# RMS norm with its sums on every partition, the norm of the next chunk begun at tile 2, and three id lists in place of one

## The chip, the cores and the metric

One Trainium2 chip, one core of it. The metric is the device time of one execution in microseconds (us), lower is better.

TensorE does the matmuls; VectorE, ScalarE and GpSimd (POOL in the profile) the elementwise work; SyncE (SP) issues most of the DMAs, POOL the indirect ones. Each of them works through its own instructions in order.

## What is computed

The input x has 8 batches of 3072 tokens with 256 features. Three blocks follow one another; cut to what matters:

```python
X = np.fft.rfft(x, axis=1)                       # Fourier block, per batch
Yr = Xr @ w_r - Xi @ w_i + b_r
Yi = Xr @ w_i + Xi @ w_r + b_i
Y = soft_threshold(Yr, 0.01) + 1j * soft_threshold(Yi, 0.01)
x = np.fft.irfft(Y, n=3072, axis=1)              # now 24576 tokens x 256

rms = np.sqrt(np.mean(x * x, axis=-1, keepdims=True) + 1e-06)
xn = x / rms * rms_g                             # RMS norm
x = (silu(xn @ w_gate) * (xn @ w_val)) @ w_out   # gated MLP, 1536 wide

expert_idx = np.argmax(normalize(x) @ normalize(expert_emb).T / tau, axis=1)
out[mask_e] = gate_w * (np.maximum(x[mask_e] @ w1[e], 0.0) @ w2[e])   # 8 experts, 1024 wide
```

## The kernel before, in words

Products are made in float16 with a high and a low part of each operand, so most products are three matmuls (high times high, high times low, low times high).

**Startup** prepares constants and weights and the Fourier block of batch 0. The last DMA of the Fourier block (`gen_A`) writes its result to G in memory.

**Chunk stage.** There are 64 chunks of 384 tokens (CT), 8 to a batch, c = 0 to 7. For each chunk, `load_gt` loads a piece of G, a chunk ahead. `norm_steps` makes from it, with 24 small matmuls (L819), the activations v (features on partitions, tokens along the row), squares them into q on ScalarE, adds the two halves on POOL and splits the sum into bfloat16 parts (two halves of q, and ql). The sums over features come from nine matmuls with a column of ones at L843, in `ms`; they stand with tokens on partitions. From them VectorE computes the reciprocal root on 128x3 values (m, mri, mry, mrt), two DMAs through memory (rd, then R) bring it as one row to all 128 partitions, VectorE multiplies v by R, ScalarE writes xnh and POOL xnl, the two halves of the normalized activations. v, q, R, xnh and xnl have one buffer each.

A chunk then has 12 tiles (`gv`, L887): 12 matmuls of 128x384 with xnh and xnl into two of the four PSUM banks of this kind, a SiLU on ScalarE (th), the product hf on VectorE (L154), hh on ScalarE and hl on VectorE. Three output tiles follow (`out_tile`, L921), 108 matmuls of 128x264. `route_steps` is the router of the chunk before: positions of each token among its expert's, then three indirect DMAs from POOL (L992) that scatter the 384 token ids into the list idl in memory; posi holds the places, rowi (L967) the ids. The rows themselves go to x2d.

What sets the order: `norm_steps` and `route_steps` are generators. `tick` advances both, twice in a gv tile and at each step of an output tile; `pump` advances `gen_A` of the next batch, which runs beside the chunks c = 0 to 4 of a batch (chunks with FFT work; 5 to 7 are plain). The norm of the next chunk is begun at tile f = 6:

```python
if more and f == 6:
    self.ns = self.norm_steps(*chunks[i + 1])
```

The scheduler then puts each engine's instructions in a fixed order.

**Expert stage** (`phase_C`). Twelve jobs, eight experts and four floating ones that take what is over, 52 units of work. The token ids of a unit come from idl (loads idx0, idx1, idx and fidx), an indirect DMA from POOL gathers the rows, and a transposing DMA on SP brings them into xt. The weights of a job come as w1f and w2f on SP; `gen_expert` takes their maxima on VectorE (rm, L1075 and L1078), scales and splits them. In each unit ScalarE makes eh and VectorE el from the first product; the second product is at L1164. `prep` runs beside the units: it loads job j once `self.done >= j - 3`, then makes the weights of job j - 1.

`prefill` writes a number past the last token into all of idl, early in startup (six DMAs, pfill).

## Time and profile before

| | before |
|---|---|
| runs | 4216.44, 4218.2, 4221.3 us; median 4218.2 |
| the profiled execution | 4221.03 us, its span 4219.1 us |
| granted TensorE clock, mean | 0.982 |
| startup / chunk stage / expert stage | 158.6 / 2971.8 / 1088.7 us |
| busy: TensorE | 3997.2 us (95%) |
| busy: VectorE, ScalarE, POOL | 2516.2 us (60%), 1929.2 us (46%), 1211.0 us (29%) |

The profile is of one execution. Busy time is the time in which an engine executes something; waiting instructions are not in it. A clock of 1 is the full 2.4 GHz. In the rows, L843 is line 843 of the kernel before, `out<-in` names the tiles written and read, x is a count, and a bracket behind a row holds the idle time before it and what ended it.

### The profile page before, as it was taken

To read this page: it belongs to the slowest core of one execution; us is meant where nothing else is said; L and a number is where in the kernel's file an instruction comes from. 1 tells how busy PE (TensorE), PEld (TensorE's weight loads), DVE (VectorE), ACT (ScalarE), POOL (GpSimd) and SP (SyncE) were. 2 spreads that over 40 slices of the span, in tenths; PEclk is the share of its full clock that TensorE was granted. 3 is DMA by queue.
4 is the path that set the end of the run, shared out by engine and by line. 5 is a ranking of instruction groups with operands and counts; after the bars stand their busy time and mean duration, and the time that the engine had idled before them with its cause. 6 is when DMAs were issued, how large, how long until landed. Compare 5 with 4: busy or idle time off the path is not lost.

```text
span 4219.1 us, 82489 instructions
## 1 busy us (share of the span) xinstructions
PE 3997.2 (95%) x31534; PEld 2835.7 (67%) x31534; DVE 2516.2 (60%) x7667; ACT 1929.2 (46%) x4326; POOL 1211.0 (29%) x1451
## 2 busy tenths in 40 slices
PE   8889999998999999999999999999999999999998
PEld 6566666766766676677667667666666666666666
DVE  7566577667756766676676576666663343333432
ACT  5544454455446444544544454444442333333332
POOL 3123113321322232132123213222233333333332
PEclk9899999999999999999999999999999999999999
DMA  7221122112212221321132123211124343333431
GB/s 239 61 55 45 31 52 56 44 35 56 55 33 50 60 48 30 62 50 38 41 59 52 29 43 56 77 27 29 22 58 116 91 112 95 94 91 91 95 76 46
DMA packets 337697, 263.42 MB, mean 62 GB/s; under 512 B 232789, under 2 KB 304259, under 8 KB 337298
## 3 DMA queue, kind: packets, MB, share of 16 engines
q1 hardware_dynamic: 311954, 206.39, 21.6%
q0 software_dynamic: 25344, 51.73, 4.7%
q8 instruction: 248, 4.06, 0.5%
q14 instruction: 151, 1.24, 0.1%
HBM read 133.02 MB, written 77.79 MB: 50 GB/s over the span
## 4 chain that ended last, share of the span: by engine, by line
PE 57%; DMA 16%; DVE 15%; issue 4%; ACT 4%; POOL 3%; SPq 1%; DVEq 0%; POOLq 0%; ACTq 0%
PE gv L887 21%; PE gv L1148 11%; PE ms L1164 6%; PE out L1164 6%; DMA R<-rd 5%; PE out L921 4%; DMA rd<-mry 3%; DMA idl<-rowi,posi 3%; PE ms L540 3%; DVE hf L154 3%; DVE hl L150 2%; PE gv L921 2%; ACT hh L158 1%; DMA at<-A 1%; POOL xnl L150 1%
## 5 line engine op out<-in xcount | busy, mean ns | idle before, releaser
L887 PE MATMUL gv<-xnh,wgvh 128*128 128x384 f16 x3072 | 1007.5, 328 | 52.0 <-DVE hf L154 30.3
L887 PE MATMUL gv<-xnl,wgvh 128*128 128x384 f16 x3072 | 1007.7, 328 | 22.4 <-POOL xnl L150 22.4
L887 PE MATMUL gv<-xnh,wgvl 128*128 128x384 f16 x3072 | 1007.6, 328 | 0.0
L887 PEld LDWEIGHTS <-wgvh 128*128 128x128 f16 x6144 | 586.3, 98 | 431.3 <-issue 79.5
L158 ACT ACTIVATE hh<-hf 128x384 f16<-128x384 f32 x768 | 400.6, 522 | 629.3 <-DVE hf L154 628.1
L150 DVE TENSOR_TENSOR hl<-hf,hh 128x384 f16<-128x384 f32 x768 | 461.3, 601 | 282.3 <-ACT hh L158 279.6
L921 PEld LDWEIGHTS <-hh 128*128 128x128 f16 x4608 | 455.0, 99 | 74.1 <-issue 0.5
L154 DVE SCALAR_TENSOR_TENSOR hf<-gv,kh,th 128x384 f32<-128x384 f32 x768 | 469.7, 612 | 35.0 <-PE gv L887 22.4
L1148 PE MATMUL gv<-xt,w1h 128*128 128x512 f16 (+1 forms) x1664 | 484.2, 375 | 0.8 <-ACT w1h L158 0.8
L992 POOL DMA_INDIRECT idl<-rowi,posi x192 | 204.4, 1064 | 970.4 <-DMA idl<-rowi,posi 398.8
L158 ACT ACTIVATE th<-gv,kg 128x384 f32<-128x384 f32 x768 | 435.3, 568 | 59.1 <-PE gv L887 58.6
L887 PEld LDWEIGHTS <-wgvl 128*128 128x128 f16 x3072 | 301.0, 98 | 235.3 <-issue 41.2
L154 DVE SCALAR_TENSOR_TENSOR el<-gv,eh 128x512 f16<-128x512 f32 (+1 forms) x416 | 276.5, 669 | 282.9 <-ACT eh L158 282.9
L921 PE MATMUL out<-woh,hl 128*128 128x264 f16 x1536 | 428.8, 279 | 0.4 <-DVE hl L150 0.4
L921 PE MATMUL out<-woh,hh 128*128 128x264 f16 x1536 | 429.1, 279 | 0.0
L921 PE MATMUL out<-wol,hh 128*128 128x264 f16 x1536 | 428.9, 279 | 0.0
L158 ACT ACTIVATE eh<-gv 128x512 f16<-128x512 f32 (+1 forms) x416 | 240.8, 580 | 284.9 <-PE gv L1148 284.2
L1164 PEld LDWEIGHTS <-eh 128*128 128x128 f16 x3200 | 313.4, 98 | 56.7 <-issue 0.6
L1170 POOL DMA_INDIRECT out<-o,xg x200 | 202.1, 1010 | 487.1 <-ACT o L158 239.5
L1148 PE MATMUL gv<-xt,w1l 128*128 128x512 f16 (+1 forms) x832 | 311.0, 374 | 0.0
L150 POOL TENSOR_TENSOR xnl<-v,xnh 128x384 f16<-128x384 f32 x128 | 116.2, 928 | 662.3 <-ACT xnh L158 637.6
L1148 PEld LDWEIGHTS <-w1h 128*128 128x128 f16 x1664 | 163.8, 99 | 147.2 <-issue 5.4
(339 smaller groups left out, 7462.4 us busy)
## 6 DMA issues: line engine op xcount, KB each, us to landing
x2d<-row SPq DMA_DIRECT2D x64, 387.0 KB, 5.8
G<-go SPq DMA_DIRECT2D x192, 128.0 KB, 1.8
gt<-G SPq DMA_DIRECT2D x64, 384.0 KB, 4.5
xc<-in_x SPq DMA_DIRECT2D x60, 384.0 KB, 6.0
R<-rd SPq DMA_DIRECT2D x64, 192.0 KB, 4.2
w1f<-in_moe_w SPq DMA_DIRECT2D x12, 1024.0 KB, 9.5
w2f<-in_moe_w SPq DMA_DIRECT2D x12, 1024.0 KB, 6.5
xt<-xg SPq DMA_TRANSPOSE x200, 3.2
```

The costliest lines, as they stand in the source:

```text
L150: (eng or self.nc.vector).tensor_tensor(out=out, in0=a, in1=b, op=op)
L154: self.nc.vector.scalar_tensor_tensor(out=out, in0=a, scalar=s, in1=b, op0=op0, op1=op1)
L158: self.nc.scalar.activation(out=out, in_=a, func=func, **kw)
L540: nc.tensor.matmul(ps, lhsT=x[u][z][:, dc], rhs=W[w][:, dc, z * D:z * D + D], start=(k == 0), stop=(k == 11))
L887: nc.tensor.matmul(p_, lhsT=self.wgv[q][u][:, dc, f * P:(f + 1) * P], rhs=xn[w][:, dc], start=(k == 0), stop=(k == 5))
L921: nc.tensor.matmul(ps, lhsT=a[:, k * P:(k + 1) * P], rhs=w[:, f], start=(n == 0), stop=(n == 3 * NF - 1))
L992: nc.gpsimd.indirect_dma_start(out=self.idl, out_offset=bass.IndirectOffsetOnAxis(ap=pi[:, k:k + 1], axis=0), in_=ri[:, k:k + 1], in_offse ...
L1148: nc.tensor.matmul(ps, lhsT=w1[1 + a][:, dc, f * P:(f + 1) * P], rhs=xt[:, 2 * z + dc, 0:n], start=(k == 0), stop=(k == 5))
L1164: nc.tensor.matmul(ps, lhsT=a[:, f, k * P:(k + 1) * P], rhs=w2[1 + z][:, f], start=(j == 0), stop=(j == 3 * NFE - 1))
L1170: nc.gpsimd.indirect_dma_start(out=self.out, out_offset=bass.IndirectOffsetOnAxis(ap=xg[:, k, 257:258], axis=0), in_=o, in_offset=None, bo ...
```

## The change

Four parts. The sums over features come from three matmuls of a 128x128 matrix of ones with the 128x384 squares, so that each partition holds the sum of every token; the reciprocal root is then computed on 128x384 values, and the two DMAs through memory fall away. The norm of the next chunk begins at tile 2, in the last chunk of a batch still at tile 6. The id list becomes three, one for each of the scatters; whoever reads ids loads from all three and takes the least. Prefill is moved to the end of startup, and `prep` loads the weights of a job without waiting for `done`, and waits with the making of job j - 1 until `done >= j - 4`.

```diff
@@ -822,58 +822,50 @@
             yield 1
             yield 1
         self.tt(q[:, 0], q[:, 0], q[:, 1], ALU.add, nc.gpsimd)
-        for _ in range(5):
-            yield 1
-        ps = self.ps("ms")
-
-        def by_k(a):
-            return a.rearrange("p (n k) -> p n k", k=3)
-
-        qh = [q[:, i].bitcast(BF16).rearrange("p (n k t) -> p n k t", k=3, t=2)[:, :, :, 1] for i in range(2)]
-        ql = pb.tile([P, CT], BF16, tag="ql", name="ql", bufs=1)
-        self.tt(by_k(q[:, 1]), by_k(q[:, 0]), qh[0], ALU.subtract, nc.gpsimd)
-        yield 1
-        yield 1
-        self.tt(by_k(ql), by_k(q[:, 1]), qh[1], ALU.subtract, nc.gpsimd)
         for _ in range(3):
             yield 1
-        parts = qh + [by_k(ql)]
-        for k in range(3):
-            for i, z in enumerate(parts):
-                nc.tensor.matmul(ps[:, k:k + 1], lhsT=z[:, :, k], rhs=self.onesb[:, 0:1], start=(i == 0), stop=(i == 2))
+
+        qh = [q[:, i].bitcast(BF16).rearrange("p (n t) -> p n t", t=2)[:, :, 1] for i in range(2)]
+        ql = pb.tile([P, CT], BF16, tag="ql", name="ql", bufs=1)
+        self.tt(q[:, 1], q[:, 0], qh[0], ALU.subtract, nc.gpsimd)
+        for _ in range(2):
+            yield 1
+        self.tt(ql, q[:, 1], qh[1], ALU.subtract, nc.gpsimd)
+        for _ in range(6):
+            yield 1
+
+        ps = self.ps("ms")[:, 0:CT]
+        for i, z in enumerate(qh + [ql]):
+            nc.tensor.matmul(ps, lhsT=self.onesb, rhs=z, start=(i == 0), stop=(i == 2))
         yield 1
-        m = self.sm(pb, "m", 3)
-        self.ts(m, ps[:, 0:3], self.eb[b], 1e-30, ALU.add, ALU.max)
+        m, t = q[:, 0], q[:, 1]
+        self.ts(m, ps, self.eb[b], 1e-30, ALU.add, ALU.max)
         yield 1
-        y = yield from self.one(self.rsqrt_steps(pb, m, 3, "mr"))
-        self.ts(y, y, 32768.0)
+
+        y = pb.tile([P, CT], F32, tag="R", name="R", bufs=1)
+        nc.vector.tensor_scalar(out=t.bitcast(I32), in0=m.bitcast(I32), scalar1=1, scalar2=None, op0=ALU.logical_shift_right)
         yield 1
-
-        rd = self.rd[(b * NCH + c) % 2]
-        nc.sync.dma_start(out=rd.rearrange("(p k) -> p k", k=3), in_=y)
-        R = pb.tile([P, CT], F32, tag="R", name="R", bufs=1)
-        nc.sync.dma_start(out=R, in_=rd.unsqueeze(0).broadcast_to([P, CT]))
-        for _ in range(4):
+        nc.vector.tensor_scalar(out=y.bitcast(I32), in0=t.bitcast(I32), scalar1=-1.0, scalar2=1597463007.0, op0=ALU.mult, op1=ALU.add)
+        yield 1
+        for _ in range(3):
+            self.tt(t, y, y)
+            yield 1
+            self.stt(t, t, -0.5, m, ALU.mult, ALU.mult)
+            yield 1
+            self.stt(y, t, 1.5, y, ALU.add, ALU.mult)
             yield 1
         xh = pb.tile([P, 2, CT], F16, tag="xnh", name="xnh", bufs=1)
         xl = pb.tile([P, 2, CT], F16, tag="xnl", name="xnl", bufs=1)
         for dc in range(2):
-            self.tt(v[:, dc], v[:, dc], R)
+            self.stt(v[:, dc], v[:, dc], 32768.0, y, ALU.mult, ALU.mult)
             yield 1
         for dc in range(2):
             self.act(xh[:, dc], v[:, dc])
+            yield 1
+        for dc in range(2):
             self.tt(xl[:, dc], v[:, dc], xh[:, dc], ALU.subtract, nc.gpsimd)
-            yield 1
         self.xn[b, c] = (xh, xl)
-
-    def one(self, g):
-
-        while True:
-            try:
-                next(g)
-            except StopIteration as e:
-                return e.value
-            yield 1
+        yield 1
 
     def gv(self, b, c, f):
         nc, pb = self.nc, self.pb
@@ -990,7 +982,7 @@
         nc.vector.tensor_copy(pi, ps_)
         for k in range(3):
             nc.gpsimd.indirect_dma_start(
-                out=self.idl, out_offset=bass.IndirectOffsetOnAxis(ap=pi[:, k:k + 1], axis=0),
+                out=self.idl[k], out_offset=bass.IndirectOffsetOnAxis(ap=pi[:, k:k + 1], axis=0),
                 in_=ri[:, k:k + 1], in_offset=None)
         yield
         y = yield from self.rsqrt_steps(pb, ssx, 3, "rx")
@@ -1043,17 +1035,28 @@
 
         nc = self.nc
         n = -(-(NE * self.CAP + FUNIT) // (6 * P)) * 6 * P
-        self.idl = self.dram.tile([n, 1], I32, name="idl")
+
+        self.idl = [self.dram.tile([n, 1], I32, name=f"idl{k}") for k in range(3)]
         self.x2d = self.dram.tile([self.NT + 1, ROW], I32, name="x2d")
         w = n // P
         t = pf.tile([P, 512], F32, tag="dq", name="pfill", bufs=2)[:, 0:w // 6].bitcast(I32)
         nc.gpsimd.memset(t, self.NT)
-        for j in range(6):
-            nc.sync.dma_start(out=self.idl.rearrange("(j p w) o -> j p (w o)", p=P, j=6)[j], in_=t)
+        for l in self.idl:
+            for j in range(6):
+                nc.sync.dma_start(out=l.rearrange("(j p w) o -> j p (w o)", p=P, j=6)[j], in_=t)
         z = pf.tile([1, ROW], I32, name="zrow")
         nc.gpsimd.memset(z, 0)
         nc.gpsimd.memset(z[:, ROW - 1:ROW], BIGID)
         nc.sync.dma_start(out=self.x2d[self.NT:self.NT + 1], in_=z)
+
+    def load_ids(self, pool, name, shape, src, bufs=1):
+
+        t = [pool.tile([P] + shape, I32, tag=f"{name}{k}", name=f"{name}{k}", bufs=bufs) for k in range(3)]
+        for o, l in zip(t, self.idl):
+            self.nc.sync.dma_start(out=o, in_=src(l))
+        for k in (1, 2):
+            self.tt(t[0], t[0], t[k], ALU.min)
+        return t[0]
 
     def expert(self, pw, w1src, w2src):
 
@@ -1114,8 +1117,7 @@
 
         n = EARLY * UNIT
         self.ts(self.cntb[:, 0:1], self.cntb[:, 0:1], float(n), op0=ALU.max)
-        idx = self.pw.tile([P, n // P], I32, name="idx0")
-        self.nc.sync.dma_start(out=idx, in_=self.idl[0:n].rearrange("(p k) o -> p (k o)", p=P))
+        idx = self.load_ids(self.pw, "idx0", [n // P], lambda l: l[0:n].rearrange("(p k) o -> p (k o)", p=P))
         n4 = UNIT // P
         self.early = [self.unit_load(self.pw, idx[:, n4 * k:n4 * k + n4], n4) for k in range(EARLY)]
 
@@ -1236,21 +1238,20 @@
 
         nc = self.nc
         p0 = nc.sync.value_load(self.tb[0:1, col], min_val=0, max_val=NE * self.CAP)
-        idx = pc.tile([P, FUNIT // P], I32, tag="fidx", name="fidx", bufs=bufs)
-        nc.sync.dma_start(out=idx, in_=self.idl[bass.ds(p0, FUNIT)].rearrange("(p k) o -> p (k o)", p=P))
-        return idx
+        return self.load_ids(pc, "fidx", [FUNIT // P], lambda l: l[bass.ds(p0, FUNIT)].rearrange("(p k) o -> p (k o)", p=P), bufs=bufs)
 
     def phase_C(self, pc, pw, w0, w1):
         nc = self.nc
         spp = self.SLOT // P
         per = self.SLOT // UNIT
         n4 = UNIT // P
-        idl = self.idl[0:NE * self.CAP].rearrange("(e r) o -> e (r o)", e=NE)
         lo = EARLY * UNIT
-        idx0 = pc.tile([P, spp - lo // P], I32, name="idx1")
-        nc.sync.dma_start(out=idx0, in_=idl[0, lo:self.SLOT].rearrange("(p k) -> p k", p=P))
-        idx = pc.tile([P, NE - 1, spp], I32, name="idx")
-        nc.sync.dma_start(out=idx, in_=idl[1:NE, 0:self.SLOT].rearrange("e (p k) -> p e k", p=P))
+
+        def by_expert(l):
+            return l[0:NE * self.CAP].rearrange("(e r) o -> e (r o)", e=NE)
+
+        idx0 = self.load_ids(pc, "idx1", [spp - lo // P], lambda l: by_expert(l)[0, lo:self.SLOT].rearrange("(p k) -> p k", p=P))
+        idx = self.load_ids(pc, "idx", [NE - 1, spp], lambda l: by_expert(l)[1:NE, 0:self.SLOT].rearrange("e (p k) -> p e k", p=P))
 
         jobs = []
         for e in range(NE):
@@ -1289,11 +1290,11 @@
             yield
             for j in range(2, len(jobs) + 1):
                 if j < len(jobs):
-                    while self.done < j - 3:
-                        yield
                     load_w(j)
                     yield
                 if j > 2:
+                    while self.done < j - 4:
+                        yield
                     yield from self.gen_expert(pw, ws[j - 1])
                     self.ready = j - 1
 
@@ -1363,13 +1364,13 @@
         self.ns = sa
         for _ in range(3):
             next(ga)
-        self.prefill(wp)
         for _ in ga:
             pass
         for _ in self.rs:
             pass
         for _ in self.load_c(False):
             pass
+        self.prefill(wp)
         self.rate = None
 
     def main(self):
@@ -1378,7 +1379,6 @@
         self.hpend = None
         self.ns = self.rs = self.xs = iter(())
         self.rcred, self.rate = 0.0, None
-        self.rd = [self.dram.tile([CT], F32, name=f"rd{i}") for i in range(2)]
         self.G = [self.dram.tile([96, T2, 512], F16, name=f"G{b}") for b in range(2)]
         es = ExitStack()
         self.pa = es.enter_context(tc.tile_pool(name="pa", bufs=1, side="right"))
@@ -1446,7 +1446,7 @@
                 if more and edge and f == 3:
                     drain(ga)
                     self.load_gt(*chunks[i + 1])
-                if more and f == 6:
+                if more and f == (6 if edge else 2):
                     self.ns = self.norm_steps(*chunks[i + 1])
                 self.gv(b, c, f)
                 pump(1.95 * rg)
```

On POOL, the router's scatters of a plain chunk of the first batch and the norm that shares the chunk with them (row writes the token number, rowi the ids, q and ql the squares, xnl the low half of the activations). Before:

```order
L1018 TENSOR_SCALAR row<-kr 128x3
L992 DMA idl<-rowi,posi 211200x1 x3
L967 TENSOR_SCALAR rowi<-kr 128x3
L150 TENSOR_TENSOR q<-q 128x384 x2
L150 TENSOR_TENSOR ql<-q 128x384
L150 TENSOR_TENSOR xnl<-v,xnh 128x384 x2
```

and now:

```order
L1010 TENSOR_SCALAR row<-kr 128x3
L150 TENSOR_TENSOR q<-q 128x384
L984 DMA idl_1245<-rowi,posi 211200x1
L150 TENSOR_TENSOR q<-q 128x384
L984 DMA idl_1246<-rowi,posi 211200x1
L984 DMA idl_1247<-rowi,posi 211200x1
L150 TENSOR_TENSOR ql<-q 128x384
L959 TENSOR_SCALAR rowi<-kr 128x3
L150 TENSOR_TENSOR xnl<-v,xnh 128x384 x2
```

The first q stands ahead of the scatters, the second among them, and ql ahead of rowi.

On VectorE, gv tiles 7 to 9 of the fourth chunk of the second batch (c and at, yv and yw belong to the FFT of the batch after). Before:

```order
L154 SCALAR_TENSOR_TENSOR hf<-gv,kh,th 128x384
L154 SCALAR_TENSOR_TENSOR c_81<-ms,c_81 128x4x128
L150 TENSOR_TENSOR hl<-hf,hh 128x384
L144 TENSOR_SCALAR c_81<-c_81 128x8x64
L154 SCALAR_TENSOR_TENSOR hf<-gv,kh,th 128x384
L144 TENSOR_SCALAR at<-at,eq 128x1024
L150 TENSOR_TENSOR hl<-hf,hh 128x384
L154 SCALAR_TENSOR_TENSOR yv<-ms,k_8555,bsc_8551 128x256
L146 TENSOR_SCALAR yw<-yv,lam,nlam 128x256
L154 SCALAR_TENSOR_TENSOR hf<-gv,kh,th 128x384
```

and now, from the second of these hf to the third:

```order
L154 SCALAR_TENSOR_TENSOR hf<-gv,kh,th 128x384
L154 SCALAR_TENSOR_TENSOR q<-q 128x384
L144 TENSOR_SCALAR at<-at,eq 128x1024
L154 SCALAR_TENSOR_TENSOR yv<-ms,k_8424,bsc_8420 128x256
L154 SCALAR_TENSOR_TENSOR R<-q,R 128x384
L146 TENSOR_SCALAR yw<-yv,lam,nlam 128x256
L150 TENSOR_TENSOR q<-R 128x384
L150 TENSOR_TENSOR hl<-hf,hh 128x384
L154 SCALAR_TENSOR_TENSOR hf<-gv,kh,th 128x384
```

Three wide operations of the reciprocal root (q, R, q) stand between two hf that had none of them between.

On SP, the beginning of the expert stage, weight loads against the transposes of the units (xt; ISA rows are bookkeeping). Before:

```order
L1132 DMA_TRANSPOSE xt<-xg 128x4x128 x20
L1064 DMA w1f<-in_moe_w 128x2x1024
L1064 DMA w2f<-in_moe_w 128x8x256
L1132 DMA_TRANSPOSE xt<-xg 128x4x128 x18
L1064 ISA
L1064 DMA w1f<-in_moe_w 128x2x1024
L1132 DMA_TRANSPOSE xt<-xg 128x4x128 x4
L1064 ISA
L1064 DMA w2f<-in_moe_w 128x8x256
```

and now:

```order
L1067 DMA w1f<-in_moe_w 128x2x1024
L1067 DMA w2f<-in_moe_w 128x8x256
L1134 DMA_TRANSPOSE xt<-xg 128x4x128 x20
L1067 ISA
L1067 DMA w1f<-in_moe_w 128x2x1024
L1067 ISA
L1067 DMA w2f<-in_moe_w 128x8x256
L1134 DMA_TRANSPOSE xt<-xg 128x4x128 x26
```

The loads of the same job stand twenty transposes earlier, and the pair that was split by four transposes stands together.

## Rows read from the trace of the kernel before

**Rows 1.** Busy by stretch: length, busy us PE, PEld, DVE, ACT, POOL; clock, DMA share, GB/s.

```profile
158.61:3130.45 2971.84, 2815.45 (x23652) 2027.84 (x23652) 1976.19 (x6394) 1460.47 (x3449) 776.71 (x977) 0.98 0.21 45
3130.45:4219.10 1088.65, 1055.10 (x7321) 716.09 (x7318) 429.47 (x959) 383.77 (x703) 388.37 (x394) 0.99 0.37 91
635.50:697.60 62.10, 57.15 (x508) 41.92 (x506) 41.36 (x128) 25.32 (x62) 18.58 (x24) 0.95 0.27 57
```

**Rows 2.** What TensorE waits for: total us, times, longest us.

```profile
PE gv L887 <- DVE hf L154: 30.3, 35, 2.8
PE ms L843 <- POOL q L150: 26.0, 22, 5.2
PE gv L887 <- POOL xnl L150: 22.4, 60, 0.7
PE out L1164 <- DVE el L154: 20.9, 7, 7.1
PE ms L843 <- POOL ql L150: 17.2, 26, 0.9
PE gv L887 <- ACT xnh L158: 12.9, 5, 8.6
PE ms L540 <- DVE go L154: 12.4, 6, 2.3
PE ms L511 <- DVE go L154: 12.2, 10, 4.2
...
PE ms L511 <- DVE at L144: 7.8, 2, 7.5
```

**Rows 3.** Timeline of POOL in a plain chunk: start us, duration, instruction, [idle before, releaser].

```profile
2718.82 0.96 POOL L992 DMA_INDIRECT idl<-rowi,posi  x1 [6.19 <-DMA idl<-rowi,posi]
2723.43 0.22 POOL L967 TENSOR_SCALAR rowi<-kr 128x3 int32<-128x3 int32 x1 [3.65 <-DMA idl<-rowi,posi]
2723.63 1.88 POOL L150 TENSOR_TENSOR q<-q 128x384 f32<-128x384 f32 x2
```

**Rows 4.** Timeline of TensorE in the same stretch.

```profile
2724.66 0.21 PE L843 MATMUL ms<-onesb,q 128*128 128x1 bf16 x1 [5.21 <-POOL q L150]
```

**Rows 5.** Timeline of VectorE in the output stage of a chunk with FFT work.

```profile
792.92 1.03 DVE L150 TENSOR_TENSOR v<-v,R 128x384 f32<-128x384 f32 x2 [4.36 <-DMA R<-rd]
```

**Rows 6.** Timeline of TensorE in the same stretch.

```profile
794.34 0.38 PE L540 MATMUL ms<-wh,c 128*128 128x256 f16 x2 [2.15 <-DVE go L154]
```

**Rows 7.** Chain that ended last, one piece: start us, us, what.

```profile
813.43 7.82 PE gv L887 x48
```

**Rows 8.** Timeline of TensorE: first of nine sums, and what follows.

```profile
871.34 0.21 PE L843 MATMUL ms<-onesb,q 128*128 128x1 bf16 x2
...
871.68 0.27 PE L921 MATMUL out<-woh,hh 128*128 128x264 f16 x1
```

**Rows 9.** VectorE groups by shape: form, count, busy us, mean ns, idle before them.

```profile
L154 DVE SCALAR_TENSOR_TENSOR hf<-gv,kh,th 128x384 f32<-128x384 f32 x768 | 469.7, 612 | 35.0 <-PE gv L887 22.4 <-ACT th L158 5.5 <-PE ms L558 0.6
...
L150 DVE TENSOR_TENSOR v<-v,R 128x384 f32<-128x384 f32 x128 | 66.2, 555 | 308.1 <-DMA R<-rd 308.1
...
L87 DVE TENSOR_TENSOR mrt<-mry 128x3 f32<-128x3 f32 x192 | 33.7, 175 | 5.6
...
L574 DVE TENSOR_SCALAR wgvf<-dq 128x512 uint32<-128x512 uint32 x12 | 5.3, 438 | 0.1
```

**Rows 10.** Tile ql: duration ns least, median, most.

```profile
L150 POOL TENSOR_TENSOR ql<-q x64: 825/827/1152, 144.1 to 3080.4; 128x384 bf16<-128x384 f32 x64
```

**Rows 11.** Timeline of VectorE in the expert stage.

```profile
3417.66 1.28 DVE L1078 TENSOR_REDUCE rm<-w2f 128x2 f32<-128x512 f32 x2 [7.90 <-DMA w2f<-in_moe_w]
```

**Rows 12.** Timeline of TensorE in the expert stage.

```profile
3419.59 0.28 PE L1164 MATMUL out<-w2h,el 128*128 128x256 f16 x1 [3.94 <-DVE el L154]
```

**Rows 13.** Chain that ended last, startup: start us, us, what.

```profile
22.41 6.34 DMA idl<-pfill
```

**Rows 14.** Timeline of SP's queue in startup.

```profile
21.89 3.99 SPq L1052 DMA_DIRECT2D idl<-pfill  x6
```

## The prediction

> **What bounds the kernel now.** I read the busy time by stage first. In the chunk stage (the 64 chunks of the gated MLP) TensorE works 2815.45 of 2971.84 us, in the expert stage 1055.10 of 1088.65 us, both at a granted clock of 0.98 or more, TensorE's 2.4 GHz level almost throughout [rows 1]. TensorE is the bound; a change can win only its idle time, some 156 us in the chunk stage and 34 us after it, and pays in full for each matmul that it adds. VectorE is the next engine: 1976.19 us in the chunk stage, 41.36 of 62.10 us in a chunk that also carries the FFT of the next batch [rows 1].
>
> So the second view is what TensorE waits for [rows 2]. The norm's sums (L843) wait for POOL's q and ql, 26.0 + 17.2 = 43.2 us. The first tile of a chunk waits for xnl 22.4 us and for xnh 12.9 us (8.6 of it once, in chunk 0). The FFT matmuls at L540 and L511 wait for VectorE's go and at, 12.4 + 12.2 + 7.8 = 32.4 us. The waits for hf, 30.3 us, are VectorE behind in the gv tiles. In the expert stage the waits for el are 20.9 us.
>
> Two timelines say why. On POOL, in a plain chunk, a scatter of ids into the one list stands 6.19 us until the scatter before it has landed, and rowi, which reuses the buffer the scatter reads, 3.65 us more; only then do the two q operations run, up to the moment at which L843, after 5.21 us, gets its first operand [rows 3, 4]. On VectorE, in the output stage of a chunk with FFT work, v stands 4.36 us until the broadcast R has landed; go, which is ready, is queued behind it, and TensorE's L540 loses 2.15 us [rows 5, 6]. So two waits on round trips through memory hold in-order engines, and other work is late behind them. The change takes away both round trips on these paths.
>
> **The change part by part**, against the profiled execution's own 4221.0 us; the median of the runs shown is 2.8 us lower.
>
> *Scatters and an earlier norm.* Each of the three scatters of a chunk now has a list of its own, so none waits for the one before; the order shows them close together with q and ql among them and ql ahead of rowi. With the norm begun at tile 2, q starts before the scatters rather than behind them. In chunks with c = 7 the start stays at tile 6. Of 43.2 us I leave 10 for those and for places where a scatter of 1 us still comes first: **-33 us** (bounds -43 and 0).
>
> *xnl and xnh.* v is ready before the output stage begins, so xnh and xnl, whose buffers come free at the last gv matmul, are made under 36 x 3 output matmuls instead of at the chunk's end. xnl 22.4 to 2: **-20** (bounds -22, 0). xnh: 4.3 us outside chunk 0 go, and in chunk 0 the two DMAs fall away but twelve wide operations with FFT work between them take nearly as long: 1 us. **-5** (bounds -13, +2).
>
> *The wait for R.* The two DMAs and VectorE's stand at v are gone. 32.4 us of go and at [rows 2] depend on it, as in [rows 5, 6]; the waits of the first batch among them (the at, 7.5 us) have other causes too, and VectorE comes to the output stage later than before (below). I take **-24** (bounds -32, 0).
>
> *TensorE's own work.* Nine 128x1 matmuls that waited for nothing took 871.34 to 871.68, 0.34 us [rows 8]. The three 128x384 that replace them cost what a gv matmul costs, 7.82 / 48 = 0.163 us [rows 7], if their strided right-hand side streams at the same rate: 64 x (3 x 0.163 - 0.34) = **+9.5 us**. No row shows a moving operand with a step of two elements; at half the rate it would be 64 x (0.98 - 0.34) = +41. I take the low end, since the nearest row has the same columns [rows 7], and keep the other.
>
> *VectorE.* Thirteen small operations of about 0.18 us (2.3 us a chunk) become twelve wide ones: three of one input at 0.44 to 0.6, three products at 0.56, six of the three-operand kind at 0.61 [rows 9], with v's two now of the last kind: some 6.6 + 0.1 us. That is +4.4 us a chunk, 280 us in all, on an engine that stood idle for R, 308.1 us over the 64 chunks [rows 9]. It is no cost by itself. But now it falls into gv tiles 7 to 11, as the order shows: between two hf stand up to three wide operations, 1.8 us beside the 1.2 of hf and hl, while a tile is 12 x 0.163 = 2.0 us of TensorE plus the FFT matmuls. A tile's PSUM banks are free for the tile two later once hf is done, so about one tile of lag is covered, and a chunk has five to eight tiles to take it up. In chunks c = 2, 3 and 4 of a batch, where FFT work on VectorE stands in the same tiles, I count 0.5 us for each of 21 chunks and a little elsewhere: **+12** (bounds 0 and +53, 1.5 us in each of the 35 chunks with FFT work). In the output stage, which begins with VectorE later: **+3** (0 to +10).
>
> *Expert stage.* VectorE stood 7.90 us for w2f, el was late behind it and TensorE lost 3.94 us [rows 11, 12]. Weights are now asked for as soon as buffers allow, ahead of transposes on SP that they stood behind; the maxima (rm) of each expert come when done allows. But twelve loads of float ids instead of four now stand ahead of the third job's weights on SP, and three lists are joined by two small minima each. Of 20.9 us I take **-9** (bounds -20, +6).
>
> *Startup.* Six prefill DMAs, 3.99 us of SP and 6.34 us in the chain that ends at the first matmuls [rows 13, 14], leave the beginning; eighteen come on SP at the end of startup, 18 x 0.67 = 12 us, among stores of go for which SP waits anyway. **-1** (-6 to +8).
>
> Sum: -33 - 20 - 5 - 24 + 9.5 + 12 + 3 - 9 - 1 = -67.5. 4221.0 - 67.5 = 4153.5 profiled, less 2.8: **4150 us** for the median.
>
> **The rivals.** A difference of 0.2%, 8.4 us, is about what a measurement of this kernel can tell from no change.
>
> *One: the waits move on.* rowi still stands for the last scatter's landing, and what follows it on POOL is xnl; if q of the next chunk is also caught behind a scatter, TensorE waits at the new sums for what it waited for at L843. For: POOL stood idle 3.65 us at rowi alone [rows 3]. Against: the order has q ahead of rowi. Then the -33 are gone, and some of xnl: 4150 + 33 + 10 = 4193 us. 0.10.
>
> *Two, slower: VectorE overruns.* The place is gv tiles 7 to 11 of the 35 chunks with FFT work. If the lag passes what two tiles' banks cover, each microsecond of the added 4.4 lands on TensorE as a wait for hf: 35 x 2.5 = 88 us in place of 12, and the gain of 24 behind R is eaten by the lag too: 4150 + 76 + 24 = 4250 us. It decides once such a chunk's VectorE share, 41.36 of 62.10 us before and 45.8 now, is concentrated: above 95% through the five tiles. For: hf is already the largest single wait [rows 2]. Against: over the chunk the share is only 0.74, and the idle time at R goes. 0.09.
>
> *Three: POOL and VectorE shut each other out.* A POOL operation that runs beside VectorE would be stretched by it. Measured: ql on POOL takes 825 ns at least, 827 in the median, 1152 at most, in a stage where VectorE is busy two thirds of the time [rows 1, 10], so mostly by nothing, at worst by 0.33 us. If instead the new 280 us of VectorE work were held up for the 776.71 / 2971.84 = 0.26 of the time in which POOL works, 73 us, 35/64 of it in the chunks where VectorE decides, that is +40: 4190 us. 0.05. The Trainium skill (SBUF — State Buffer, section "SBUF: two separate sides") has such a rule: a VectorE operation with two SBUF inputs and a GpSimd operation that reads SBUF take one shared port pair as an exclusive lock, and the later one blocks fully. All nine products of the new root have two SBUF inputs, so it speaks against this change; the trace's durations of ql do not show it, though a block before the start would not be in a duration.
>
> *Four: half-rate streaming* of the strided squares, +31: 4181 us. 0.06.
>
> **How the numbers follow.** Forecast 0.70, rivals 0.10, 0.09, 0.05 and 0.06. Forecast and rivals one, three and four end under 4209.8 (faster by over 0.2%), though their outer parts do not: faster 0.84, same 0.07, slower 0.09. The range takes the bounds of the large terms, which will not all fall on one side (about 30 us down from the forecast), and upward the rivals up to 4193: 4118 to 4202 us.
>
> **What would show it.** Right: the waits for q and ql at the new sums under 12 us in all; no idle time before scatters by another scatter; xnl and xnh under 10 us; go and at under 12; three sums taking about 0.5 us; VectorE near 2790 us busy; el near 12. Wrong: a group of waits for hf well above 45 us (rival two), POOL still idle for landing ids with TensorE waiting behind (one), POOL operations of 1.2 us or idle time of VectorE ended by POOL (three), sums of 0.33 us each (four).

## The result and the profile after

| | before | after |
|---|---|---|
| median of the runs, us | 4219.75 (4216.44 to 4227.05) | 4158.17 (4153.01 to 4160.71) |
| ratio to before | | 0.9848 (95% interval 0.9836 to 0.986) |
| profiled execution / span, us | 4221.03 / 4219.1 | 4153.01 / 4151.2 |
| granted TensorE clock, mean | 0.982 | 0.986 |

The forecast was 4150 us with a range of 4118 to 4202. The first line below is the page's busy time of each engine, the three after it are the busy time by stretch (startup, chunk stage, expert stage; columns as in [rows 1]).

```profile
PE 3980.2 (96%) x31150; PEld 2821.6 (68%) x31150; DVE 2763.4 (67%) x7617; ACT 1938.4 (47%) x4326; POOL 1225.7 (30%) x1451
0.00:155.19 155.19, 125.26 (x557) 90.76 (x558) 112.83 (x313) 84.34 (x175) 46.07 (x81) 0.91 0.67 202
155.19:3073.48 2918.29, 2803.23 (x23274) 2014.23 (x23274) 2220.64 (x6334) 1471.51 (x3449) 792.44 (x979) 0.99 0.17 42
3073.48:4151.20 1077.72, 1051.73 (x7320) 716.65 (x7318) 429.89 (x971) 382.58 (x703) 387.18 (x391) 0.99 0.37 91
```

The chunk stage is 53.5 us shorter (2971.84 to 2918.29), the expert stage 10.9, startup 3.4; together the 67.9 us of the span. The gain has two sorts. TensorE's idle time fell by 50.9 us (221.9 to 171.0 over the span). Its *busy* time fell too, from 3997.2 to 3980.2 us, though the three wide sums keep it busy 48.0 us where the nine small ones took 39.0. So all its other matmuls together are some 26 us less busy. Matmuls that ran slowly, most of them at the lower clock, account for some 15 of these (counted below), and the prediction had no term for that; where the rest went no view shows.

What TensorE waits for now (total us, times, longest us):

```profile
PE gv L879 <- DVE hf L154: 40.5, 43, 3.0
PE ms L839 <- POOL q L150: 20.1, 17, 2.3
PE ms L967 <- DVE go L154: 18.6, 6, 3.1
PE gv L1150 <- DVE el L154: 8.9, 5, 3.5
PE ms L511 <- DVE c L154: 7.9, 6, 1.3
PE ms L839 <- POOL ql L150: 6.3, 13, 0.6
PE ms L540 <- ACT q L158: 6.2, 6, 1.5
...
PE ms L511 <- DVE at L144: 5.5, 2, 5.3
...
PE gv L879 <- ACT xnh L158: 3.9, 1, 3.9
...
PE out L1166 <- DVE el L154: 2.8, 2, 2.1
...
PE gv L879 <- ACT th L158: 2.3, 10, 0.3
PE gv L879 <- POOL xnl L150: 1.7, 5, 0.9
```

Against [rows 2]: xnl 22.4 to 1.7, xnh 12.9 to 3.9, el 20.9 to 8.9 + 2.8. The waits for go at L540 and L511 (24.6 us) are gone, and the one for at is 5.5. The sums, now L839, still wait 26.4 us where L843 waited 43.2. And three lines are new: L967, the router's position sums, 18.6 us for go; L511 for c, 7.9; L540 for ScalarE's q, 6.2.

By a count from the trace, 29.5 of the 40.5 us for hf stand in chunks c = 2 (before, 22.1 of 30.3), and 15.8 of the sums' 26.4 in chunks c = 4.

Two kinds of chunk show where the waits come from. In c = 3 the norm, begun at tile 2, has its matmuls and its small work in the same tiles as the router and the FFT (TensorE's timeline; six batches show the same two waits):

```profile
1056.58 0.38 PE L540 MATMUL ms<-wh,c 128*128 128x256 f16 x2 [0.93 <-ACT q L158]
...
1061.14 0.18 PE L967 MATMUL ms<-oh,kh 128*128 128x32 f16 x1 [3.09 <-DVE go L154]
```

In c = 4 POOL has the scatters and rowi ahead of q. The scatters no longer wait for one another (POOL's idle time before them for a landing scatter fell from 398.8 to 0.6 us), but rowi, whose buffer the last of them reads, stands 6.77 us, and q behind it (POOL's timeline, then TensorE's from the sums on):

```profile
1491.43 1.01 POOL L984 DMA_INDIRECT idl<-rowi,posi  x1 [0.30 <-issue]
1499.21 0.23 POOL L959 TENSOR_SCALAR rowi<-kr 128x3 int32<-128x3 int32 x1 [6.77 <-DMA idl<-rowi,posi]
1499.41 1.89 POOL L150 TENSOR_TENSOR q<-q 128x384 f32<-128x384 f32 x2
```

```profile
1498.33 0.33 PE L879 MATMUL gv<-xnh,wgvl 128*128 128x384 f16 x1
1500.45 0.33 PE L839 MATMUL ms<-q,onesb 128*128 128x384 bf16 x1 [1.79 <-POOL q L150]
1501.35 0.48 PE L839 MATMUL ms<-q,onesb 128*128 128x384 bf16 x1 [0.57 <-POOL q L150]
1502.25 0.48 PE L839 MATMUL ms<-ql,onesb 128*128 128x384 bf16 x1 [0.43 <-POOL ql L150]
1502.53 0.53 PE L879 MATMUL gv<-xnh,wgvh 128*128 128x384 f16 x1
1502.85 0.53 PE L879 MATMUL gv<-xnl,wgvh 128*128 128x384 f16 x1
...
1507.33 0.52 PE L879 MATMUL gv<-xnh,wgvh 128*128 128x384 f16 x1
...
1507.85 0.33 PE L879 MATMUL gv<-xnh,wgvl 128*128 128x384 f16 x1
1508.01 0.33 PE L879 MATMUL gv<-xnh,wgvh 128*128 128x384 f16 x1
```

The waits at the three sums are 1.79, 0.57 and 0.43 us. Behind them the gv matmuls start 0.32 us apart, from 1502.53 to 1507.33, where they stood 0.16 apart before the wait and do so again from 1507.85: after 2.8 us of waits TensorE ran at 1.2 GHz instead of 2.4 for some 5 us (granted clock 0.50 from 1502.53 to 1507.33, 1.00 from 1507.85 on). Sixteen matmuls at 0.16 us too much are 2.5 us, nearly the waits once more. By a count from the two traces, matmuls of the chunk stage that took over 1.45 times their usual step, with no idle time of TensorE straight behind them, lost 44.5 us before and 33.9 after (63.0 and 47.6 over the whole span). So at a place like this one, a wait that goes takes part of its own length with it a second time; that every slow stretch follows from the waits before it is not shown.

VectorE's new work (groups by shape: busy us, mean ns, idle before):

```profile
L150 DVE TENSOR_TENSOR q<-R 128x384 f32<-128x384 f32 x192 | 106.9, 557 | 3.6
L154 DVE SCALAR_TENSOR_TENSOR q<-q 128x384 f32<-128x384 f32 x192 | 106.3, 554 | 2.8
...
L154 DVE SCALAR_TENSOR_TENSOR v<-v,R 128x384 f32<-128x384 f32 x128 | 66.4, 551 | 1.0
...
L146 DVE TENSOR_SCALAR q<-ms,eb 128x384 f32<-128x384 f32 x64 | 39.0, 610 | 22.8 <-PE ms L839 22.7
...
L846 DVE TENSOR_SCALAR q<-q 128x384 int32<-128x384 int32 x64 | 22.6, 354 | 1.1
```

The wide operations cost 0.55 to 0.61 us, as taken, and 0.35 to 0.36 for the two on integers; VectorE is busy 2763.4 us for 2516.2. Three sums that wait for nothing take 1007.70 to 1008.21, 0.51 us, so the strided squares stream at the full rate:

```profile
1007.70 0.50 PE L839 MATMUL ms<-q,onesb 128*128 128x384 bf16 x2
1008.04 0.32 PE L839 MATMUL ms<-ql,onesb 128*128 128x384 bf16 x1
1008.21 0.32 PE L879 MATMUL gv<-xnh,wgvh 128*128 128x384 f16 x1
```

### The profile page after: what moved, and what is told of

It reads as the page before. It is cut to its first block, busy times and chain, and to the rows that moved or that the text cites. A ratio compares the mean times of both kernels' runs of the same rounds, so it can differ in the third digit from the quotient of the medians.

```text
span 4151.2 us, 81518 instructions
## 1 busy us (share of the span) xinstructions
PE 3980.2 (96%) x31150; PEld 2821.6 (68%) x31150; DVE 2763.4 (67%) x7617; ACT 1938.4 (47%) x4326; POOL 1225.7 (30%) x1451
## 5 line engine op out<-in xcount | busy, mean ns | idle before, releaser
L879 PE MATMUL gv<-xnh,wgvh 128*128 128x384 f16 x3072 | 1013.2, 330 | 48.2 <-DVE hf L154 40.5
L150 DVE TENSOR_TENSOR hl<-hf,hh 128x384 f16<-128x384 f32 x768 | 470.1, 612 | 161.6 <-ACT hh L158 158.5
L1150 PEld LDWEIGHTS <-w1h 128*128 128x128 f16 x1664 | 163.2, 98 | 154.2 <-issue 12.5
```

The costliest lines, as they stand in the source:

```text
L150: (eng or self.nc.vector).tensor_tensor(out=out, in0=a, in1=b, op=op)
L879: nc.tensor.matmul(p_, lhsT=self.wgv[q][u][:, dc, f * P:(f + 1) * P], rhs=xn[w][:, dc], start=(k == 0), stop=(k == 5))
L1150: nc.tensor.matmul(ps, lhsT=w1[1 + a][:, dc, f * P:(f + 1) * P], rhs=xt[:, 2 * z + dc, 0:n], start=(k == 0), stop=(k == 5))
```

## The experiments

Twelve kernels ran, in three groups of four. The kernel before ran with each group, and took 4250, 4181 and 4259 us (medians of 7 runs each), where it had 4219.75 beside the changed kernel. Kernels are therefore compared within a group, by their medians or by their ratios to the kernel before of that group; across groups only what is read inside the profiles is compared (lengths of chunks, waits), and a microsecond of a chunk's length says nothing there: the changed kernel's own chunks c = 3 and c = 4 took 58.4 and 55.4 us in its first profile, 57.5 and 54.4 in that of the second group. A chunk's length below is the mean over batches two to seven, from its first gv matmul to that of the next chunk.

The changed kernel itself did not run in the first group. `u_gate`, which differs from it in the expert stage alone, stands for its chunk stage there: 2923.4 us.

### First group: one part undone

**The norm at tile 6 everywhere** (`u_late`).

```diff
-                if more and f == (6 if edge else 2):
+                if more and f == 6:
```

> The changed kernel with the norm of the next chunk begun at tile 6 again in every chunk; all else as changed. Theory (the early start is what puts q ahead of the scatters and of rowi on POOL): the waits of the sums for q and ql go from 26 us up to about 40, the sums and the twelve wide operations fall into the output stage; the waits that the early start brought (L967 for go 18.6 us, L540 for q 6.2 us) go. About 4165 us, between 4158 and 4175. Rival (the early start alone hides xnl and xnh): 20 to 30 us of these waits come back too, 4185 us or more.

Measured: 4134.18 us, ratio 0.9735 (0.9718 to 0.9752), the second fastest of the group; the changed kernel with only the load gate put back (`u_gate`) took 4170.44 in it, and its chunk stage is 25 us longer than the 2898.3 here. So undoing the early start makes the kernel *faster*. Both expectations fell. The waits:

```profile
PE gv L879 <- DVE hf L154: 51.2, 35, 4.5
...
PE gv L879 <- POOL xnl L150: 2.7, 7, 0.7
...
PE ms L839 <- POOL q L150: 2.4, 2, 2.0
```

With three lists and without the round trip through R, xnl (2.7 us) and the sums (2.4 us) do not need the early start. The new waits at L967 and at L540 for q are not in its list. Others are longer in their place: hf 51.2 us (42.3 of them in c = 2), th 19.5 for 2.3, and go at L558 10.7, which the changed kernel's list does not have. A chunk c = 3 takes 54.1 us for 57.8 in `u_gate`, c = 4 51.6 for 56.0; c = 2 is longer, 64.5 for 61.7, and c = 0 and 1 by 0.6 and 0.7 us. The early start wins in these three kinds of chunk and loses more in c = 3 and 4.

**One id list again** (`u_onelist`), with the loads of before and six prefill DMAs at the end of startup.

```diff
-                out=self.idl[k], out_offset=bass.IndirectOffsetOnAxis(ap=pi[:, k:k + 1], axis=0),
+                out=self.idl, out_offset=bass.IndirectOffsetOnAxis(ap=pi[:, k:k + 1], axis=0),
```

> The changed kernel with one id list again (one scatter waits for the one before, two fewer loads per reader, no minima, six prefill DMAs, at the end of startup). Theory (three lists and early start do the same job twice: q now stands ahead of most scatters): POOL stands some 400 us for landing scatters again, the sums wait some 10 us more, 4163 to 4170 us. Rival (the lists carry the gain): the 43 us of before come back, 4175 us or more. Second rival (lists do nothing for TensorE): 4158 us.

Measured: 4130.12 us, ratio 0.9728 (0.9708 to 0.9747): 40 us under the kernel with the gate put back, 30 of them in the chunk stage (2893.3 for 2923.4). No expectation had a gain. A chunk c = 4 takes 51.7 us, and the sums wait 3.4 + 5.8 us instead of 20.1 + 6.3. Since a scatter then has to wait for the one before, the scheduler puts q between the scatters there and rowi last; with three lists it puts all three scatters and rowi first. The lists took a wait from POOL (it stands 311.6 us between scatters here) and gave TensorE another by the order.

**The gate on the weight loads** (`u_gate`).

```diff
                 if j < len(jobs):
+                    while self.done < j - 3:
+                        yield
                     load_w(j)
                     yield
                 if j > 2:
-                    while self.done < j - 4:
-                        yield
```

> The changed kernel with the weight loads of job j again held until done >= j - 3, and no wait before the making of the weights. Theory (the gate makes el late): the waits for el go from 11.7 back to about 21 us, 4167 us. Rival (the twelve id loads or the buffers set the time, not the gate): 4158 us.

Measured: 4170.44 us (0.9817). Its waits for el are 16.5 + 2.8 = 19.3 us for 11.7, as expected; the time from the last output matmul of the chunk stage to the end is 1088.6 us in it and 1074.6 to 1078.5 in the other three of the group. The gate costs 10 to 14 us. The edit takes back both lines of this part, the earlier loads and the later making of the weights; no run parts the two.

**The memory round trip** (`u_norm`): `norm_steps` of before, begun at tile 2.

```diff
-            nc.tensor.matmul(ps, lhsT=self.onesb, rhs=z, start=(i == 0), stop=(i == 2))
+                nc.tensor.matmul(ps[:, k:k + 1], lhsT=z[:, :, k], rhs=self.onesb[:, 0:1], start=(i == 0), stop=(i == 2))
...
+        nc.sync.dma_start(out=rd.rearrange("(p k) -> p k", k=3), in_=y)
+        nc.sync.dma_start(out=R, in_=rd.unsqueeze(0).broadcast_to([P, CT]))
```

> The changed kernel with the sums, the small root and the two DMAs through memory of before, the norm still begun at tile 2. Theory (VectorE's stand at R costs through what is queued behind it): VectorE stands some 250 to 300 us for R again, waits for go, at and hf grow by 30 to 45 us, TensorE saves 9.5 us of matmuls and some lag of VectorE: 4175 to 4190 us. Rival (with the early start the round trip is hidden, and the wide root only adds work): 4145 us, faster than the changed kernel.

Measured: 4224.4 us (0.9942), 54 us above the kernel with the gate put back (its chunk stage is 64 us longer) and more above the changed kernel. VectorE stands for R again (VectorE's waits):

```profile
DVE v L150 <- DMA R<-rd: 263.0, 62, 7.3
```

The waits of the sums are 37.1 + 9.1 us in it, for xnh and xnl 20.1. The theory held, with a larger size; the rival, that the early start hides the round trip, fell. Undone by itself, this part costs the most of the four; by itself on the kernel before it brings less (`a_norm`, below). L967's wait for go stands here too, at L975, 18.6 us: the early start brings it, with the small root as with the wide one.

### Second group: one part alone, and the ids from a table

**The changed kernel once more** (`after_again`), as the group's measure.

> The changed kernel itself, to stand beside the others on the same chip: 55 to 85 us under the kernel before.

Measured: 4138.3 us, ratio 0.9904 (0.9888 to 0.9921): 43 us under the kernel before, less than expected. Against the first measurement the kernel before took 39 us less and the changed kernel 20 us less; why is not known.

**The wide norm alone on the kernel before** (`a_norm`): `norm_steps` of the change.

```diff
-                nc.tensor.matmul(ps[:, k:k + 1], lhsT=z[:, :, k], rhs=self.onesb[:, 0:1], start=(i == 0), stop=(i == 2))
+            nc.tensor.matmul(ps, lhsT=self.onesb, rhs=z, start=(i == 0), stop=(i == 2))
```

> The kernel before with the wide norm alone (three sums, root on 128x384, no memory round trip), begun at tile 6, one id list, the expert stage as before. Theory (the round trip through R is the largest part of the gain): the waits for go, at and xnl and what the clock loses after them go, the waits of the sums stay where scatters are ahead: 45 to 70 us under the kernel before. Rival (it needs the early start, or VectorE's added 4.4 us a chunk cost what is won): within 15 us of the kernel before.

Measured: 4155.98 us, ratio 0.994 (0.9924 to 0.9957), 25 us under: between the two expectations. Its sums wait 13.3 + 9.6 us, hf 46.6, and go at L558 13.4 (4.1 before). xnl is down to 2.3 us, with one list and the old start: the wide norm alone ends this wait.

**Three lists alone on the kernel before** (`a_lists`), with the change's loads, minima and eighteen prefill DMAs.

```diff
-                out=self.idl, out_offset=bass.IndirectOffsetOnAxis(ap=pi[:, k:k + 1], axis=0),
+                out=self.idl[k], out_offset=bass.IndirectOffsetOnAxis(ap=pi[:, k:k + 1], axis=0),
```

> The kernel before with the three id lists alone (and prefill with 18 DMAs in its early place). Theory (rowi still stands for the last scatter, ahead of q): POOL's stand between scatters goes, some 400 us, but the waits of the sums fall only from 43 to about 25 us, some 15 to 20 us under the kernel before. Rival (the lists take the whole wait away, as the prediction had it): 33 us or more under it, with what the clock gives back. Second rival (more loads and minima cost as much): no difference.

Measured: 4157.61 us, ratio 0.9946 (0.9927 to 0.9966), 23 us under, between the theory and the rival. The mechanism was the rival's, the waits of the sums go almost whole (TensorE's waits, the only line on L843):

```profile
PE ms L843 <- POOL q L150: 2.0, 1, 2.0
```

rowi still stands for landing ids, 196.7 us in all, but with the scatters early and together that is over before TensorE needs q. Part of what the kernel gives back lies in startup: the chunk stage starts at 163.2 us, where it starts at 153 to 159 in all the others, and the early prefill takes SP ten microseconds more, eighteen DMAs in one row of SP's timeline where [rows 14] has six:

```profile
21.93 13.95 SPq L1054 DMA_DIRECT2D idl<-pfill  x18
```

The waits for xnl stay (16.9 us). Alone, the wide norm and the lists bring about the same, 25 and 23 us of the 43, and they do not simply add up with the other two parts.

**Ids from a table** (`i_rows`). On the changed kernel, the ids of all chunks are written once in startup, so no rowi stands on POOL:

```diff
-        ri = self.sm(pb, "rowi", 3, I32)
-        nc.gpsimd.tensor_scalar(out=ri, in0=self.krow, scalar1=float(r0), scalar2=None, op0=ALU.add)
+        ri = self.rows[:, 3 * (b * NCH + c):3 * (b * NCH + c) + 3]
```

> The changed kernel with the ids of all chunks written once at the start (a table of 192 columns), so that no rowi stands on POOL. Theory (in chunks c = 4 q is queued behind rowi, which stands for the scatters just issued): the waits of the sums for q fall from 20 to under 8 us, the loss to the low clock in c = 4 from 12 to about 3 us: 15 to 25 us under the changed kernel. Rival (q is late there because the scatters themselves, or their descriptors, hold POOL): within 5 us of it.

Measured: 4114.22 us, ratio 0.9845 (0.9828 to 0.9861): 24 us under the changed kernel of the group, as the theory had it. A chunk c = 4 takes 50.9 us for 54.4, and the slow matmuls of all eight of them (counted as above) lose 0.7 us for 6.7. The rival fell: with the scatters still there, q is in time. With 0.9845 against 0.9904 this version beats both kernels on the same ground. The sums (now L845) wait 2.5 us; the router's wait for go stays (now L972):

```profile
PE ms L972 <- DVE go L154: 18.6, 6, 3.1
...
PE ms L845 <- POOL q L150: 2.5, 2, 2.0
```

### Third group: what is left

**The norm at tile 6 in c = 3** (`i_mix`), on top of the table.

```diff
-                if more and f == (6 if edge else 2):
+                if more and f == (6 if edge or c == 3 else 2):
```

> The changed kernel with the table of ids and with the norm begun at tile 6 in chunks c = 3 as well as c = 7. Theory (in c = 3 the early start puts the norm's matmuls and small sums in the way of the FFT's: L967 waits 3.1 us for go, L540 0.9 us for q, and the clock falls after it): a chunk c = 3 takes 54 to 55 us instead of 58.5, 20 to 28 us in all, about 2.2% under the kernel before of the same chip. Rival (the waits only move into the output stage): a chunk c = 3 stays at 57 us or more and the whole at 1.5% under it.

Measured: 4111.56 us, ratio 0.9661 (0.964 to 0.9682). A chunk c = 3 takes 53.7 us for 58.5, and the waits at L967 and L540 for q are gone. The whole is 148 us under the kernel before of its group, but hardly under the table's 4114 of the other group: in all four kernels of this group the last chunk takes 46 to 50 us, for 38 to 40 in the changed kernel and with the table, with TensorE idle 4.1 to 6.8 us in waits of its output matmuls that no engine ends. Here are those of `i_mix` (TensorE's waits); among and behind them the granted clock is 0.50 for 10 us, from 3013.9 to 3024.2:

```profile
PE out L919 <- issue: 5.3, 4, 1.7
```

Whether these belong to this program or to the group was not tried.

**Tile 4 in c = 3** (`i_rows4`).

```diff
-                if more and f == (6 if edge else 2):
+                if more and f == (6 if edge else 4 if c == 3 else 2):
```

> The same with tile 4 in chunks c = 3. Theory: any start that keeps the squares' matmuls out of the tiles in which the router's position sums stand does it, 54 to 56 us for a chunk c = 3. Rival (it is the place of the sums, not of the start): 57 us or more.

Measured: 4117.92 us, 0.9675 (0.9653 to 0.9697), a chunk c = 3 54.5 us. Either later start does it.

**Two Newton steps** (`i_two`), on `i_mix`.

```diff
-        for _ in range(3):
+        for _ in range(2):
             self.tt(t, y, y)
```

> The first of these kernels with two Newton steps of the reciprocal root instead of three: three wide VectorE operations fewer in each chunk, 106 us of VectorE work in all; the root is less exact, since the third step is left out. Theory (VectorE's added work is hidden except in the few chunks with FFT work): 3 to 12 us faster. Rival (VectorE decides in the gv tiles): 25 us or more faster.

Measured: 4091.64 us (4085.29 to 4096.87), ratio 0.9617 (0.9596 to 0.9639), 20 us under `i_mix`, between the two expectations. VectorE is busy 2666.4 us for 2761.9 and TensorE idle 70.6 us in the chunk stage for 88.7. The two pages' rows:

```profile
PE 3960.5 (96%) x31150; PEld 2817.5 (69%) x31150; DVE 2761.9 (67%) x7617; ACT 1930.0 (47%) x4326; POOL 1217.9 (30%) x1394
```

```profile
PE 3958.7 (97%) x31150; PEld 2818.3 (69%) x31150; DVE 2666.4 (65%) x7425; ACT 1927.3 (47%) x4326; POOL 1225.7 (30%) x1394
```

So 95 us of VectorE work fewer gave back 20 us of time, a fifth of it.

**One list on top of the table** (`i_one`), on `i_mix`, with the loads and the prefill of `u_onelist`.

```diff
-                out=self.idl[k], out_offset=bass.IndirectOffsetOnAxis(ap=pi[:, k:k + 1], axis=0),
+                out=self.idl, out_offset=bass.IndirectOffsetOnAxis(ap=pi[:, k:k + 1], axis=0),
```

> The first of these kernels with one id list again, filled by six DMAs at the end of startup. Theory (with rowi gone nothing that TensorE waits for stands behind the scatters' landing): POOL stands some 300 us between scatters, and the time stays within 6 us; two fewer loads per reader make the expert stage 2 to 4 us shorter. Rival (the stand between scatters reaches q, xnl or the FFT's yw): 10 us or more slower.

Measured: 4113.99 us, 0.9668 (0.9647 to 0.9689), 2.4 us from `i_mix`, although POOL stands between scatters again (POOL's group of scatters):

```profile
POOL idl L989 <- DMA idl<-rows,posi: 279.8, 106, 5.7
```

With rowi gone and q in time, one list does as well as three. The part after the last output matmul is 1073.0 us for 1077.1, the upper end of the 2 to 4 us that the theory gave to the fewer loads.

## Why the prediction was right, and where its sum was wrong

The profiled execution, the fastest of its four runs, fell by 68.0 us where the sum said 67.5; the median fell by 61.6, to 4158.17 us where 4150 was forecast. Both are closer than the terms were: errors of both signs cancelled, and that was luck.

- **The sums' waits, -33 said, -16.8 measured** (43.2 to 26.4). The step that failed: "the order shows them close together with q and ql among them and ql ahead of rowi". That was read in a plain chunk; in c = 4 the order has the scatters and rowi first, and rival one's mechanism stands there. `i_rows` shows it, and the size: 24 us with the clock. It takes both parts of the change: with three lists and the old start the sums wait 2.4 us (`u_late`), with one list and the early start 9.2 (`u_onelist`).
- **xnl -20 said, -20.7; xnh -5 said, -9.0.** The sizes are near, the reason was wrong: the prediction gave them to the early start, but `u_late` has xnl at 2.7 us without it, and `a_norm` at 2.3 with the wide norm alone. Of xnh's 9.0, 4.7 fell in chunk 0 (8.6 to 3.9), where 1 was said.
- **The wait for R, -24 said.** The old waits fell by more, 32.4 to 5.5 us for go and at. But the new ones in c = 3 and c = 2 (18.6 + 7.9 + 6.2 = 32.7) took it back, and no term had them. The step that failed is that the norm's earlier start was priced as a gain only, while its squares hold up L540 and its POOL and VectorE work falls among the router's. `u_late` and `i_mix` show it for c = 3; for the 7.9 us of c in c = 2 `u_late` has 3.6.
- **TensorE's own work, +9.5 said.** 64 x (0.51 - 0.34) = +10.9, and by its busy time at the sums 38.95 to 48.03, +9.1; rival four is out.
- **VectorE, +12 and +3 said.** The waits for hf rose by 10.2 us, 30.3 to 40.5. They grew in c = 2 (22.1 to 29.5) and fell in c = 3 and 4, which the term named with it. By `i_two` a fifth of the added work, 247 us, would be some 50 us; that is an estimate from the last 95 us of it, and the interval of the two ratios leaves room for half. So the term may have been too low; no run shows its whole size. The overrun of rival two did not come.
- **The expert stage, -9 said.** The waits for el fell by 9.2 us, the stage by 10.9. `u_gate` puts some 10 us on the gate.
- **Startup, -1 said, -3.4 measured.**
- **The clock, not in the sum.** Busy time fell by 17.0 us with some 9 us added at the sums, 26 us elsewhere; slow matmuls are 15 of these (63.0 to 47.6 us). It paid for part of what the first and third points lost.

Of the signs that the prediction named for being right, the sums' waits (26.4 us for under 12) and those for go and at (24.1 with L967, for under 12) did not come; the other five did.

Of the rivals, the first was there in part. The third was read on the wrong engine. POOL's ql is not stretched, but VectorE's operations are: in c = 3, beside POOL's two q and ql, se takes 0.99 us, gw 0.65 and row 0.88, and each ends with the POOL operation beside it, while the reciprocal between them takes its usual 0.17 (VectorE's timeline, then POOL's):

```profile
1057.97 0.99 DVE L144 TENSOR_SCALAR se<-se 128x3 f32<-128x3 f32 x1
1059.00 0.17 DVE L1025 RECIPROCAL gw<-se 128x3 f32<-128x3 f32 x1
1059.20 0.65 DVE L150 TENSOR_TENSOR gw<-gw,nrm 128x3 f32<-128x3 f32 x1
1059.89 0.88 DVE L144 TENSOR_SCALAR row<-gw,ko 128x3 f32<-128x3 f32 x1
```

```profile
1057.95 1.89 POOL L150 TENSOR_TENSOR q<-q 128x384 f32<-128x384 f32 x2 [0.26 <-ACT q L158]
1059.92 0.82 POOL L150 TENSOR_TENSOR ql<-q 128x384 bf16<-128x384 f32 x1
```

The usual times of the three are 0.16, 0.16 and 0.23 us, so they lose 0.83 + 0.49 + 0.65 = 2.0 us. go is queued behind them with pauses of 0.03 us at most, so about 2 of L967's 3.09 us come from here: an estimate, no run took the POOL operations out and left the rest. Over the whole run the loss is small: by a count from the traces, VectorE operations lose 41 us before and 56 after where they take over 0.1 us more than usual and end with a POOL operation. The Trainium skill (SBUF — State Buffer, "SBUF: two separate sides") describes such a lock, and says that whichever of the two engines comes second waits; the trace agrees in se and gw, which start behind the POOL operation; row starts 0.03 us before ql by the records and is held all the same. Of the three only gw has the two SBUF inputs that the page's rule names beside its two-port modes; which sort the other two are no run here shows.

## What to carry to other kernels

A round trip through memory ahead of an in-order engine costs what is queued behind it, and TensorE can pay for a wait again in slow matmuls behind it (2.5 us behind 2.8 in c = 4): price it together with those that follow such waits in the rows. An earlier start and a dropped dependence both move work in the order; look at the order in every kind of chunk, since each of the two here lost in some kinds more than it won in the others. A cheap operation such as rowi, whose one buffer a DMA still reads, can hold an in-order engine for a whole DMA landing: a table written once ended that.

## What the runs showed of the hardware that was not expected

- The kernel before took 4181 to 4259 us in different groups of runs, 1.9% apart, while its runs within one group lay within 0.4%. The changed kernel took 4138 and 4158 us in two groups. What differed between the groups is not known. A time without the kernel before beside it says little here.
- A gv matmul starts 0.16 us after the one before at the 2.4 GHz level and 0.32 us at 1.2 GHz, and the lower level came inside a chunk, behind waits like the 1.79, 0.57 and 0.43 us above.
- A VectorE operation of 0.16 us took up to 1.0 us beside a POOL operation, and the profile counts that as busy, not as idle.
